# Attention scores as one float32 product each, from undivided queries and keys, in a kernel of attention, an MLP and a mixture of experts

## The chip, the cores and the metric

The kernel runs on one core of one Trainium2 chip. The metric is the device time of one execution in microseconds (us), the median of several runs. The engines are called as the profile calls them: PE (TensorE; PEld are its weight loads), DVE (VectorE), ACT (ScalarE), POOL (GpSimd) and SP (SyncE, which issues the DMAs).

## The reference

```python
# attention: q, k, v of (4, 8, 576, 64): batch, heads, positions, head width
scores = q @ k.transpose(0, 1, 3, 2) / np.sqrt(64)
scores = np.where(block_i >= block_j, scores, -1e9)      # blocks of 64 positions
attn = np.exp(scores - scores.max(-1, keepdims=True))
attn = attn / (attn.sum(-1, keepdims=True) + 1e-9)
x = (attn @ v).transpose(0, 2, 1, 3).reshape(2304, 512)
# MLP
h = x @ w_in                                             # 512 -> 2048
x = np.maximum(0.01 * h, h) @ w_out                      # 2048 -> 512
# mixture of 8 experts, every token through every expert
P = sinkhorn(np.exp(x @ w_gate - max))                   # 8 rounds, (2304, 8)
out = sum(P[:, e:e+1] * (np.maximum(x @ w1[e], 0) @ w2[e]) for e in range(8))
```

## The kernel before

Three stages follow one another on PE: attention, the MLP (`hidden`, `second`), and the experts (`product`, `combine`). Almost all products are made of float32r parts: an operand is divided into a high part (a rounded copy) and a low part (the rest), and a product is three matmuls: high with high, high with low, low with high. Only the transposes and the weighted sums of attention (`weigh`) and the small gate products multiply plain float32 tiles.

Attention goes through 16 pairs of heads. For each pair the queries and keys (`qraw`, `kraw`) come by DMA, and PE turns them (`turn_q`, `turn_k`, `turn_tail`: tiles `qm`, `km`, `qk_tail` in PSUM, all from one pool of three banks that the transposes `tr` of the weights share). ACT writes the high part and then DVE the low part of the turned operand: `spread` for the queries, scaled and laid out so that the two heads of a pair stand in a block diagonal (`qbdh`, `qbdl`), `split_k` for the keys (`kTh`, `kTl`). `score(p, i)` makes the scores of query block i, of both heads at once, against the first 64(i+1) keys: three matmuls into a PSUM tile `sc` (three banks), DVE takes the row maximum (`nmax`), ACT the exponentials (`ex`) with their sums. The last block, of 576 keys, is cut into two halves of 288. `normalise` scales the weights, `turn_attn` turns them (PE, then a copy `at` by ACT or DVE), and `weigh` multiplies them with the values into `av`.

The table `turns` puts beside each score of pair p+1 other work of pairs p-1 to p+3, and a scheduler that goes by a timeline model then sets the order of each engine's instructions. Between them stand the steps of `bits_steps`, which prepare the MLP's first weights on DVE, ACT and POOL (`wa`, `wb`, `wraw`).

Of the kernel before, what the change touches and what calls it, by code (L numbers as in the profile page):

```python
# [8 lines left out]
F32 = mybir.dt.float32  # L9
F32R = mybir.dt.float32r  # L10
U32 = mybir.dt.uint32
AF = mybir.ActivationFunctionType
ALU = mybir.AluOpType
AX = mybir.AxisListType

P = 128
BLK = 64
# [10 lines left out]
def f32(ap):  # L28
    return ap.bitcast(F32)
# [7 lines left out]
def block_attention_mlp_moe(  # L37
# [15 lines left out]
    nc = tc.nc  # L53
    B, H, S, D = q.shape
# [3 lines left out]
    NQ = S // BLK  # L58
# [7 lines left out]
    TAIL = S - NFULL * P  # L66
# [151 lines left out]
    def attention(att, ps_sc, ps_tr, ps_av):  # L218
# [1 line left out]
        kraw = att.tile([P, NKC, P], F32, name="kraw")  # L220

        vraw = [att.tile([P, NKC, P], F32, name=f"vraw{i}") for i in range(2)]
        qbd = [[att.tile([P, NQ, P], F32R, name=f"qbd{n}{i}") for n in "hl"] for i in range(2)]
        kT = [[att.tile([P, S], F32R, name=f"kT{n}{i}") for n in "hl"] for i in range(2)]
        nch = [(i + 2) // 2 for i in range(NQ)]
        off = [P * sum(nch[:i]) for i in range(NQ)]
        ew = P * sum(nch)
# [36 lines left out]
        W = NFULL * P  # L264

        def spread(p, src, lo, n):
            qh, ql = qbd[p % 2]
            scale = 1.0 / float(D) ** 0.5
            for h in range(2):
                r = slice(h * D, (h + 1) * D)  # L270
                to = (r, slice(lo, lo + n), slice(h * BLK, (h + 1) * BLK))
                x = src[r, 0:n * BLK].rearrange("p (n c) -> p n c", c=BLK)
                nc.scalar.activation(out=qh[to], in_=x, func=AF.Copy, scale=scale)  # L273
                nc.vector.scalar_tensor_tensor(
                    out=ql[to], in0=x, scalar=scale, in1=f32(qh[to]), op0=ALU.mult, op1=ALU.subtract
                )

        def split_k(p, src, lo, hi):
            kh, kl = kT[p % 2]
            nc.scalar.copy(out=kh[:, lo:hi], in_=src)  # L280
            nc.vector.tensor_tensor(out=kl[:, lo:hi], in0=src, in1=f32(kh[:, lo:hi]), op=ALU.subtract)

        def turn_q(p):
            qm = ps_tr.tile([P, 512], F32, name="qm", tag="tr")
            for t in range(NFULL):
                nc.tensor.transpose(qm[:, t * P:(t + 1) * P], qraw[:, t, :], ident)  # L286
            spread(p, qm, 0, W // BLK)

        def turn_k(p):
            km = ps_tr.tile([P, 512], F32, name="km", tag="tr")  # L290
            for t in range(NFULL):
                nc.tensor.transpose(km[:, t * P:(t + 1) * P], kraw[:, t, :], ident)
            split_k(p, km[:, 0:W], 0, W)

        def turn_tail(p):
            tail = ps_tr.tile([P, 512], F32, name="qk_tail", tag="tr")
            for s, raw in enumerate((qraw, kraw)):
                nc.tensor.transpose(
                    tail[:, s * TAIL:(s + 1) * TAIL], raw[:TAIL, NFULL, :], ident[:TAIL, :TAIL]
                )  # L300
            spread(p, tail, W // BLK, TAIL // BLK)
            split_k(p, tail[:, TAIL:2 * TAIL], W, S)

# [4 lines left out]

        def score(p, i):
            n = BLK * (i + 1)
            qh, ql = (t[:, i, :] for t in qbd[p % 2])
            kh, kl = kT[p % 2]
            cuts = [(0, n)] if n <= 512 else [(0, n // 2), (n // 2, n)]
            part = []
            nm, sm = nmax[p % 2], ssum[p % 2]
            x = col[i]
            for s, (lo, hi) in enumerate(cuts):
                sc = ps_sc.tile([P, 512], F32, name="sc", tag="sc")[:, 0:hi - lo]  # L320
                for m, (a, b) in enumerate(((qh, kh), (qh, kl), (ql, kh))):
                    nc.tensor.matmul(sc, a, b[:, lo:hi], start=m == 0, stop=m == 2)  # L322
                latest[0] = nc.vector.tensor_reduce(out=nm[:, x - s:x - s + 1], in_=sc, axis=AX.X, op=ALU.max, negate=True)  # L323
                part.append(sc)
            if len(cuts) > 1:
                nc.vector.tensor_tensor(out=nm[:, x:x + 1], in0=nm[:, x:x + 1], in1=nm[:, x - 1:x], op=ALU.min)
            for s, (lo, hi) in enumerate(cuts):
                nc.scalar.activation(  # L328
                    out=ex[p % 2][:, off[i] + lo:off[i] + hi], in_=part[s], func=AF.Exp,
                    bias=nm[:, x:x + 1], scale=1.0, accum_out=sm[:, x - s:x - s + 1],  # L330
                )
            if len(cuts) > 1:
                nc.gpsimd.tensor_tensor(out=sm[:, x:x + 1], in0=sm[:, x:x + 1], in1=sm[:, x - 1:x], op=ALU.add)
# [49 lines left out]
        def split_x(p):  # L383
# [4 lines left out]
            for u0, u1 in zip(cuts, cuts[1:]):  # L388
# [13 lines left out]
            [("cur", turn_attn, 2), ("nxt", load_v)],  # L402
            [("cur", turn_attn, 3), ("cur", weigh, 0, 0, 0), ("cur", weigh, 0, 1, 0),
             ("nxt", normalise, 0, 3), ("fol", turn_k), ("fol", turn_tail)],
            [("cur", weigh, 0, 0, 1), ("cur", weigh, 0, 1, 1)],
            [("cur", turn_attn, 4), ("cur", turn_attn, 5)],
# [4 lines left out]

        load_qk(0)
        nc.scalar.activation(out=ssum[0], in_=ident[:, 0:NQ + 1], func=AF.Exp)
        for t in qbd[0] + qbd[1]:
            nc.gpsimd.memset(f32(t), 0.0)
        for t in vraw:
            nc.gpsimd.memset(t[:, NFULL, :], 0.0)
        for t in ex:
            for i in range(0, NQ, 2):
                nc.gpsimd.memset(t[:, off[i] + BLK * (i + 1):off[i] + P * nch[i]], 0.0)  # L420
        turn_q(0)
        turn_k(0)
        turn_tail(0)
        load_qk(1)
        units = [(1, f) for f in range(FC)] + [(2, f) for f in range(2)]
        steps = []
        starts = [int(n * 1.4) for n in range(len(units))]
        for p in range(-1, NP + 1):
            who = {"prv": p - 1, "cur": p, "nxt": p + 1, "fol": p + 2}
            if p in starts:  # L430
                bits_load(*units[starts.index(p)])
            if p - 1 in starts:
                steps += bits_steps(*units[starts.index(p - 1)])
            if 0 <= p < NP:
                normalise(p, 6, 9)
            for i, beside in zip(turn_order, turns):
                if p + 1 < NP:
                    score(p + 1, i)
                for w, f, *a in beside:
                    if 0 <= who[w] < NP:  # L440
                        f(who[w], *a)
                if steps and p + 1 < NP:
                    with tc.issue_after(latest[0].ins if hasattr(latest[0], "ins") else latest[0]):
                        steps.pop(0)()
                elif steps:
                    steps.pop(0)()
            if p + 3 < NP:
                load_qk(p + 3)
# [7 lines left out]
    n = 1  # L456
# [4 lines left out]
    for g in range(0, P, 32):  # L461
        r = slice(g, g + 32)
        nc.vector.tensor_tensor(out=ident[r, r], in0=ramp[r, :], in1=turned[r, :], op=ALU.is_equal)
    w2a = ctx.enter_context(tc.tile_pool(name="w2a", bufs=1))
    with (
        tc.tile_pool(name="att", bufs=1) as att,
        tc.tile_pool(name="ps_sc", bufs=3, space=bass.MemoryType.PSUM) as ps_sc,
        tc.tile_pool(name="ps_tr", bufs=3, space=bass.MemoryType.PSUM) as ps_tr,
        tc.tile_pool(name="ps_av", bufs=1, space=bass.MemoryType.PSUM) as ps_av,
    ):  # L470
        wpools[2] = [w2a]
        attention(att, ps_sc, ps_tr, ps_av)
# [456 lines left out]
    for n in range(0, NGR, 2):  # L929
        p, e, i = groups[n]  # L930
# [74 lines left out]
```

## Time and profile before

| what | value |
|---|---|
| median of 3 runs | 2155.08 us (2152.91 to 2155.52) |
| span of the profiled execution | 2155.8 us; no other time of this execution is listed |
| mean granted clock of TensorE | 0.997 |
| busy over the span | PE 98%, PEld 87%, DVE 68%, ACT 43%, POOL 23% |
| attention ends, the MLP's first product | at 255.0 us |

The span runs from the first to the last instruction of one execution. Busy times of matmuls contain the time in which the array still fills and empties behind the next one, so 98% is no measure of how full the array is. Durations in the rows further down are from this one execution.

### The profile page before, as it was taken

Reading aid. Unit: us, or ns where it says so; the run is one execution under the profiler, and the core shown is the slowest. Engines: PE = TensorE matmul, PEld = TensorE weight load, DVE = VectorE, ACT = ScalarE, POOL = GpSimd, SP = SyncE. Lnnn points to the kernel's source line nnn. Section 1 sums busy time; section 2 is a strip of 40 time slices with the busy share of each in tenths; the row PEclk is TensorE's granted clock in tenths of the full one; section 3 lists DMA queues with packets and bytes.
Section 4 is the critical chain, followed back from the end, with each engine's and each line's share of the span. In section 5 each row is a group of like instructions: output and inputs, shape, how many; then the busy total and the mean of one; then the engine's idle time right before and its main releaser. Section 6 shows DMA issues by size and latency. Waiting matters only on the chain.

```text
span 2155.8 us, 29413 instructions
## 1 busy us (share of the span) xinstructions
PE 2119.0 (98%) x10932; PEld 1865.1 (87%) x10932; DVE 1458.1 (68%) x2411; ACT 926.7 (43%) x1932; POOL 503.7 (23%) x589
## 2 busy tenths in 40 slices
PE   7989899999999999999999999999999999999999
PEld 5666688988899899899989988998899899989998
DVE  7888675653456866766678667666768676667665
ACT  6777522232334433443345344434444444344432
POOL 3344321110022212221222122212222221222120
PEclk9999999999999999999999999999999999999999
DMA  4333123230012122212222222122213221222120
GB/s 102 85 88 91 38 69 94 71 118 1 1 30 69 47 72 78 79 51 67 79 79 77 70 79 79 42 77 78 76 43 108 79 70 48 79 79 66 52 78 30
DMA packets 157248, 146.63 MB, mean 68 GB/s; under 512 B 62640, under 2 KB 126128, under 8 KB 157104
## 3 DMA queue, kind: packets, MB, share of 16 engines
q1 hardware_dynamic: 157104, 144.75, 22.7%
q8 instruction: 86, 1.41, 0.3%
q14 instruction: 58, 0.48, 0.1%
HBM read 135.81 MB, written 8.91 MB: 67 GB/s over the span
## 4 chain that ended last, share of the span: by engine, by line
PE 93%; DVE 5%; ACT 1%; issue 0%; DMA 0%; POOL 0%; SPq 0%; ACTq 0%; DVEq 0%
PE o L798 36%; PE h_ps L744 32%; PE h_ps L519 9%; PE o L548 9%; PE sc L322 2%; PE av L378 2%; PE tr L353 2%; DVE nmax L323 1%; DVE ex L346 1%; PE qm L286 0%; DVE w1l L702 0%; ACT at L360 0%; DVE wb L184 0%; ACT ex L328 0%; ACT qbdh L273 0%
## 5 line engine op out<-in xcount | busy, mean ns | idle before, releaser
L798 PE MATMUL o<-w2h,xhlate 128*128 128x512 f32 x1152 | 402.6, 390 | 0.0
L798 PE MATMUL o<-w2h,xllate 128*128 128x512 f32 x1152 | 401.6, 389 | 0.0
L685 POOL TENSOR_TENSOR wa<-wraw 128x256 f32<-128x256 f32 x96 | 89.0, 927 | 1251.3 <-DVE w1l L702 1200.5
L752 ACT COPY s<-h_ps 128x384 f32<-128x384 f32 x288 | 138.5, 481 | 540.1 <-PE h_ps L744 540.0
L761 DVE TENSOR_TENSOR c<-h_ps,s 128x384 f32<-128x384 f32 x288 | 155.6, 554 | 312.9 <-PE h_ps L744 302.6
L744 PE MATMUL h_ps<-xhS,w1h 128*128 128x384 f32 x768 | 257.1, 335 | 0.0
L744 PE MATMUL h_ps<-xlS,w1h 128*128 128x384 f32 x768 | 256.5, 334 | 0.0
L744 PE MATMUL h_ps<-xhS,w1l 128*128 128x384 f32 x768 | 256.5, 334 | 0.0
L798 PEld LDWEIGHTS o<-w2h,xllate 128*128 128x128 f32 x1152 | 216.2, 188 | 45.4
L798 PEld LDWEIGHTS o<-w2h,xhlate 128*128 128x128 f32 x1152 | 216.2, 188 | 43.4
L798 PE MATMUL o<-w2l,xhlate 128*128 128x512 f32 x576 | 224.7, 390 | 0.0
L798 PE MATMUL o<-w2l,xllate 128*128 128x512 f32 x576 | 224.4, 390 | 0.0
L811 DVE SCALAR_TENSOR_TENSOR xa<-o,pr,xa 128x512 f32<-128x512 f32 x264 | 189.1, 740 | 50.9 <-PE o L798 50.9
L744 PE MATMUL h_ps<-xhA,w1l 128*128 128x384 f32 x576 | 193.0, 335 | 0.0
L744 PE MATMUL h_ps<-xhA,w1h 128*128 128x384 f32 x576 | 193.0, 335 | 0.0
L744 PE MATMUL h_ps<-xlA,w1h 128*128 128x384 f32 x576 | 192.8, 335 | 0.0
L702 DVE TENSOR_TENSOR w1l<-wraw,w1h 128x512 fp32r<-128x512 f32 x192 | 172.9, 938 | 0.1
L702 DVE TENSOR_TENSOR w1l<-wa,w1h 128x512 fp32r<-128x512 f32 x192 | 160.8, 840 | 0.0
L767 ACT ACTIVATE xllate<-c 128x384 fp32r<-128x384 f32 x144 | 75.7, 526 | 183.7 <-DVE c L761 183.7
L132 DVE TENSOR_TENSOR w2l<-wraw,w2h 128x1024 fp32r<-128x1024 f32 x100 | 145.7, 1457 | 7.8 <-ACT w2h L131 7.8
L744 PEld LDWEIGHTS h_ps<-xlS,w1h 128*128 128x128 f32 x768 | 144.2, 188 | 0.0
L744 PEld LDWEIGHTS h_ps<-xhS,w1h 128*128 128x128 f32 x768 | 144.2, 188 | 0.0
(167 smaller groups left out, 4227.0 us busy)
## 6 DMA issues: line engine op xcount, KB each, us to landing
wraw<-in_moe_w_dram SPq DMA_DIRECT2D x192, 512.0 KB, 4.3
wraw<-in_moe_w_in_dram SPq DMA_DIRECT2D x16, 512.0 KB, 3.8
wraw<-in_moe_w_out_dram SPq DMA_DIRECT2D x16, 512.0 KB, 3.7
out_dram<-xa SPq DMA_DIRECT2D x18, 256.0 KB, 2.0
qraw<-in_q_dram SPq DMA_DIRECT2D x32, 128.0 KB, 2.5
kraw<-in_k_dram SPq DMA_DIRECT2D x32, 128.0 KB, 2.6
vraw<-in_v_dram SPq DMA_DIRECT2D x32, 128.0 KB, 2.8
s_in<-wa SPq DMA_DIRECT2D x8, 256.0 KB, 2.4
```

Of the source, the lines that this page charges most:

```text
L132: nc.vector.tensor_tensor(out=lo, in0=raw, in1=f32(hi), op=ALU.subtract)
L322: nc.tensor.matmul(sc, a, b[:, lo:hi], start=m == 0, stop=m == 2)
L519: nc.tensor.matmul(ps[:, 0:n], w[:, c, cols], x, start=c == 0 and s == 0, stop=c == KC - 1 and s == 2,)
L548: nc.tensor.matmul(o_ps[s][:, 0:n], w[:, cut], h[:, 0:n], start=f == 0 and m == 0, stop=f == FC - 1 and m == 2)
L685: nc.gpsimd.tensor_tensor(out=one[:, 0], in0=a21, in1=a22, op=ALU.add)
L702: nc.vector.tensor_tensor(out=lo, in0=x, in1=f32(hi), op=ALU.subtract)
L744: mm = nc.tensor.matmul(ps, w[:, c], x[:, c], start=first and c == 0 and s == 0, stop=c == 1 and s == 2, skip_group_check=True,)
L752: nc.scalar.copy(out=t, in_=bank[n, name][:, 0:HT])
L761: nc.vector.tensor_tensor(out=c, in0=x, in1=part[n, add], op=ALU.add)
L767: nc.scalar.activation(out=hi, in_=x, func=AF.Relu),
L798: mm = nc.tensor.matmul(o, h, w, start=m == 0, stop=m == 11)
L811: nc.vector.scalar_tensor_tensor(out=a, in0=o, scalar=pr[:, tt, e:e + 1], in1=a, op0=ALU.mult, op1=ALU.add)
```

## The change

The queries and keys are no longer divided. `qbd` and `kT` are one float32 tile each, twice, where there were a high and a low one. ACT copies the turned queries with their scale into `qbd`, DVE copies the turned keys into `kT` (`place_k`, in the place of `split_k`), and a score is one matmul of two float32 tiles.

```diff
--- before.py
+++ after.py
@@ -220,8 +220,8 @@
         kraw = att.tile([P, NKC, P], F32, name="kraw")
 
         vraw = [att.tile([P, NKC, P], F32, name=f"vraw{i}") for i in range(2)]
-        qbd = [[att.tile([P, NQ, P], F32R, name=f"qbd{n}{i}") for n in "hl"] for i in range(2)]
-        kT = [[att.tile([P, S], F32R, name=f"kT{n}{i}") for n in "hl"] for i in range(2)]
+        qbd = [att.tile([P, NQ, P], F32, name=f"qbd{i}") for i in range(2)]
+        kT = [att.tile([P, S], F32, name=f"kT{i}") for i in range(2)]
         nch = [(i + 2) // 2 for i in range(NQ)]
         off = [P * sum(nch[:i]) for i in range(NQ)]
         ew = P * sum(nch)
@@ -264,21 +264,15 @@
         W = NFULL * P
 
         def spread(p, src, lo, n):
-            qh, ql = qbd[p % 2]
             scale = 1.0 / float(D) ** 0.5
             for h in range(2):
                 r = slice(h * D, (h + 1) * D)
-                to = (r, slice(lo, lo + n), slice(h * BLK, (h + 1) * BLK))
+                to = qbd[p % 2][r, lo:lo + n, h * BLK:(h + 1) * BLK]
                 x = src[r, 0:n * BLK].rearrange("p (n c) -> p n c", c=BLK)
-                nc.scalar.activation(out=qh[to], in_=x, func=AF.Copy, scale=scale)
-                nc.vector.scalar_tensor_tensor(
-                    out=ql[to], in0=x, scalar=scale, in1=f32(qh[to]), op0=ALU.mult, op1=ALU.subtract
-                )
-
-        def split_k(p, src, lo, hi):
-            kh, kl = kT[p % 2]
-            nc.scalar.copy(out=kh[:, lo:hi], in_=src)
-            nc.vector.tensor_tensor(out=kl[:, lo:hi], in0=src, in1=f32(kh[:, lo:hi]), op=ALU.subtract)
+                nc.scalar.activation(out=to, in_=x, func=AF.Copy, scale=scale)
+
+        def place_k(p, src, lo, hi):
+            nc.vector.tensor_copy(out=kT[p % 2][:, lo:hi], in_=src)
 
         def turn_q(p):
             qm = ps_tr.tile([P, 512], F32, name="qm", tag="tr")
@@ -290,7 +284,7 @@
             km = ps_tr.tile([P, 512], F32, name="km", tag="tr")
             for t in range(NFULL):
                 nc.tensor.transpose(km[:, t * P:(t + 1) * P], kraw[:, t, :], ident)
-            split_k(p, km[:, 0:W], 0, W)
+            place_k(p, km[:, 0:W], 0, W)
 
         def turn_tail(p):
             tail = ps_tr.tile([P, 512], F32, name="qk_tail", tag="tr")
@@ -299,7 +293,7 @@
                     tail[:, s * TAIL:(s + 1) * TAIL], raw[:TAIL, NFULL, :], ident[:TAIL, :TAIL]
                 )
             spread(p, tail, W // BLK, TAIL // BLK)
-            split_k(p, tail[:, TAIL:2 * TAIL], W, S)
+            place_k(p, tail[:, TAIL:2 * TAIL], W, S)
 
 
 
@@ -310,16 +304,13 @@
 
         def score(p, i):
             n = BLK * (i + 1)
-            qh, ql = (t[:, i, :] for t in qbd[p % 2])
-            kh, kl = kT[p % 2]
             cuts = [(0, n)] if n <= 512 else [(0, n // 2), (n // 2, n)]
             part = []
             nm, sm = nmax[p % 2], ssum[p % 2]
             x = col[i]
             for s, (lo, hi) in enumerate(cuts):
                 sc = ps_sc.tile([P, 512], F32, name="sc", tag="sc")[:, 0:hi - lo]
-                for m, (a, b) in enumerate(((qh, kh), (qh, kl), (ql, kh))):
-                    nc.tensor.matmul(sc, a, b[:, lo:hi], start=m == 0, stop=m == 2)
+                nc.tensor.matmul(sc, qbd[p % 2][:, i, :], kT[p % 2][:, lo:hi], start=True, stop=True)
                 latest[0] = nc.vector.tensor_reduce(out=nm[:, x - s:x - s + 1], in_=sc, axis=AX.X, op=ALU.max, negate=True)
                 part.append(sc)
             if len(cuts) > 1:
@@ -411,8 +402,8 @@
 
         load_qk(0)
         nc.scalar.activation(out=ssum[0], in_=ident[:, 0:NQ + 1], func=AF.Exp)
-        for t in qbd[0] + qbd[1]:
-            nc.gpsimd.memset(f32(t), 0.0)
+        for t in qbd:
+            nc.gpsimd.memset(t, 0.0)
         for t in vraw:
             nc.gpsimd.memset(t[:, NFULL, :], 0.0)
         for t in ex:
```

Behind attention the instructions stand in the same order as before on all five queues. In attention the scheduler has placed them anew. On PE, the queue in the eighth pair whose tails are turned: before, with the high parts `kTh`, `qbdh` and the low parts `kTl`, `qbdl`:

```order
L322 MATMUL sc<-kTh_121,qbdh_117 128x256
L322 MATMUL sc<-kTl_122,qbdh_117 128x256
L322 MATMUL sc<-kTh_121,qbdl_118 128x256
L353 MATMUL tr<-ident,ex_126 128x128
L322 MATMUL sc<-kTh_121,qbdh_117 128x320
L322 MATMUL sc<-kTl_122,qbdh_117 128x320
L322 MATMUL sc<-kTh_121,qbdl_118 128x320
L378 MATMUL av<-at,vraw_116 64x320 x2
L378 MATMUL av<-at,vraw_116 64x192 x2
```

The same place of the changed kernel, where L313 is the score, L344 the transpose of the weights, L280 that of the queries and L369 the weighted sum:

```order
L313 MATMUL sc<-kT_119,qbd_117 128x256
L344 MATMUL tr<-ident,ex_122 128x128 x5
L280 MATMUL qm<-ident,qraw 128x128 x4
L313 MATMUL sc<-kT_119,qbd_117 128x320
L313 MATMUL sc<-kT_120,qbd_118 128x288 x2
L369 MATMUL av<-at,vraw_116 64x320 x2
L369 MATMUL av<-at,vraw_116 64x192 x2
```

Three rows have become one, and the next pair's first scores and the queries' transposes now stand ahead of the weighted sums of 320 and 192 columns. On DVE, between the scaling of the weights `ex` of one pair and the maxima of the next, before:

```order
L346 TENSOR_SCALAR ex_125<-ex_125,rsum_131 128x576
L346 TENSOR_SCALAR ex_125<-ex_125,rsum_131 128x512
L323 TENSOR_REDUCE nmax_127<-sc 128x1 x2
L281 TENSOR_TENSOR kTl_124<-km,kTh_123 128x512
L274 SCALAR_TENSOR_TENSOR qbdl_120<-qk_tail,qbdh_119 64x64
L339 RECIPROCAL rsum_131<-rsum_131 128x3
L346 TENSOR_SCALAR ex_125<-ex_125,rsum_131 128x448
L274 SCALAR_TENSOR_TENSOR qbdl_120<-qk_tail,qbdh_119 64x64
L323 TENSOR_REDUCE nmax_127<-sc 128x1 x2
L281 TENSOR_TENSOR kTl_124<-qk_tail,kTh_123 128x64
```

And in the changed kernel, where L275 is the copy of the keys, L314 the maximum, L330 the reciprocal and L337 the scaling:

```order
L337 TENSOR_SCALAR ex_121<-ex_121,rsum_127 128x576
L337 TENSOR_SCALAR ex_121<-ex_121,rsum_127 128x512
L314 TENSOR_REDUCE nmax_123<-sc 128x1
L275 COPY kT_120<-km 128x512
L314 TENSOR_REDUCE nmax_123<-sc 128x1
L330 RECIPROCAL rsum_127<-rsum_127 128x3
L275 COPY kT_120<-qk_tail 128x64
L337 TENSOR_SCALAR ex_121<-ex_121,rsum_127 128x448
L314 TENSOR_REDUCE nmax_123<-sc 128x1
```

The subtractions for `qbdl` are gone, and the copies of the keys stand where their subtractions stood.

## Rows read from the trace of the kernel before

**Rows 1.** Page, part 1: busy us, share of the span, instructions.

```profile
PE 2119.0 (98%) x10932; PEld 1865.1 (87%) x10932; DVE 1458.1 (68%) x2411; ACT 926.7 (43%) x1932; POOL 503.7 (23%) x589
```

**Rows 2.** Windows: stretch, its length, busy us (and instructions) by engine, clock.

```profile
24.20:230.00 205.80, 186.45 (x1223) 129.65 (x1222) 176.49 (x441) 158.21 (x473) 88.12 (x132) 0.98 0.33 81
122.00:136.00 14.00, 11.88 (x76) 9.47 (x76) 10.84 (x27) 9.62 (x30) 7.37 (x11) 0.88 0.30 79
...
136.00:150.00 14.00, 13.71 (x97) 9.87 (x96) 11.99 (x33) 11.38 (x35) 4.40 (x9) 1.00 0.28 64
...
262.00:300.00 38.00, 38.00 (x170) 31.45 (x169) 26.98 (x42) 12.34 (x21) 14.09 (x10) 1.00 0.24 70
```

**Rows 3.** Chain that ended last, 24.2 to 230 us, share by line.

```profile
by line: PE sc L322 18.0%; PE av L378 13.9%; PE tr L353 12.6%; DVE nmax L323 9.3%; DVE ex L346 5.6%; DVE wb L184 3.4%; ACT at L360 3.2%; DVE qbdl L274 3.0%; DVE at L362 2.9%; ACT qbdh L273 2.8%; PE qm L286 2.7%; ACT ex L328 2.5%; PE km L292
```

**Rows 4.** Waits, 24.2 to 230 us: total us, times, longest.

```profile
DVE nmax L323 <- PE sc L322: 21.1, 34, 1.7
...
PEld sc L322 <- ACT at L360: 9.3, 14, 0.7
...
ACT qbdh L273 <- DVE qbdl L274: 7.0, 8, 1.8
...
PEld av L378 <- DVE at L362: 5.9, 10, 1.1
```

**Rows 5.** Timeline of PE, 135.7 to 147.2 us: start, length, what.

```profile
137.05 0.97 PE L378 MATMUL av<-at,vraw 128*64 128x448 f32 x4
137.96 0.66 PE L353 MATMUL tr<-ident,ex 128*128 128x128 f32 x4
...
139.67 0.28 PE L322 MATMUL sc<-kTl,qbdh 128*128 128x256 f32 x1
139.79 0.27 PE L322 MATMUL sc<-kTh,qbdl 128*128 128x256 f32 x1
...
142.21 0.28 PE L322 MATMUL sc<-kTl,qbdh 128*128 128x64 f32 x1
142.32 0.28 PE L322 MATMUL sc<-kTh,qbdl 128*128 128x64 f32 x1
...
144.02 0.34 PE L378 MATMUL av<-at,vraw 128*64 128x64 f32 x4
144.28 0.33 PE L353 MATMUL tr<-ident,ex 128*128 128x128 f32 x1
...
144.68 0.40 PE L322 MATMUL sc<-kTl,qbdh 128*128 128x512 f32 x1
144.92 0.39 PE L322 MATMUL sc<-kTh,qbdl 128*128 128x512 f32 x1
```

**Rows 6.** Groups of PE up to 255 us: busy us, mean ns, idle before.

```profile
L378 PE MATMUL av<-at,vraw 128*64 128x448 f32 x128 | 31.1, 564 | 0.0
```

**Rows 7.** Groups of DVE, 24.2 to 230 us.

```profile
L274 DVE SCALAR_TENSOR_TENSOR qbdl<-qm,qbdh 64x512 fp32r<-64x512 f32 x27 | 18.5, 685 | 0.8
...
L281 DVE TENSOR_TENSOR kTl<-km,kTh 128x512 fp32r<-128x512 f32 x14 | 9.5, 677 | 0.7 <-ACT kTh L280 0.7
L362 DVE COPY at<-tr 128x512 f32<-128x512 f32 x13 | 8.9, 685 | 0.2
...
L274 DVE SCALAR_TENSOR_TENSOR qbdl<-qk_tail,qbdh 64x64 fp32r<-64x64 f32 x28 | 6.0, 214 | 1.4 <-ACT qbdh L273 0.9
```

**Rows 8.** Groups of ACT, 24.2 to 230 us.

```profile
L280 ACT CAST kTh<-km 128x512 fp32r<-128x512 f32 x14 | 8.6, 616 | 0.2 <-PE km L292 0.2
...
L280 ACT CAST kTh<-qk_tail 128x64 fp32r<-128x64 f32 x13 | 2.7, 209 | 3.2 <-DVE qbdl L274 3.1
```

**Rows 9.** Start: the memsets of line L415, and PE's first work.

```profile
L415 POOL MEMSET qbdl<- x2: 1079/1080/1082, 1.9 to 3.9; 128x1152 f32 x2
...
6.26 1.09 PE L286 MATMUL qm<-ident,qraw 128*128 128x128 f32 x4 [6.26 <-DVE ident L463]
```

**Rows 10.** The chain in order of time, 254 to 300 us.

```profile
254.98 9.52 PE h_ps L519 x41
```

## The prediction

> **What bounds the kernel now.** I began with the totals: TensorE (PE) is busy for 98% of the span, VectorE (DVE) for 68%, ScalarE (ACT) for 43% [rows 1]. That average hides two stages, so I read the windows next. From 262 us on PE is busy 38.00 of 38.00 us, DVE 26.98 and ACT 12.34; there only PE work counts, and the change touches none of it. In the attention stage, in the stretch from 24.2 to 230 us, PE is busy 186.45 of 205.8 us, DVE 176.49 and ACT 158.21 [rows 2]. No engine is at its limit there, and three are near it. So what the change is worth is decided between 0 and 255 us, and whatever time is won or lost there reaches the end unchanged, since the instructions behind attention stand in the same order on all five queues as before.
>
> Then the chain of waits in that stretch. It is shared: the score products of L322 hold 18.0% of it, the weighted sums 13.9%, the transposes 12.6%; DVE's five lines hold 9.3 + 5.6 + 3.4 + 3.0 + 2.9 = 24.2%, and ACT's three 3.2 + 2.8 + 2.5 = 8.5% [rows 3]. Of 205.8 us that is 37.0 us of scores, 49.8 us of DVE and 17.5 us of ACT. The list of waits says why DVE is in it: PE's score loads and weighted sums wait 9.3 and 5.9 us for copies by ACT and DVE, and ACT itself waits 7.0 us before the queries' high part [rows 4] and 3.1 us before that of the keys' tail [rows 8] for the low part of the queries, which DVE writes from the same PSUM tile that ACT reads. The stretch holds 14 of 16 head pairs (the 14 key tiles of 512 columns), 14.7 us each.
>
> **The change part by part.** *Score products on PE.* Before, a product is three float32r matmuls. In the stretch from 136 to 150 us, at the full clock (1.00 granted [rows 2], the 2.4 GHz level), they start 0.11 us apart at 64 columns, 0.12 at 256 and 0.24 at 512 [rows 5]: 0.47 ns a column, but never under 0.11 us. A head pair scores widths 64, 128, 192, 256, 288 (twice), 320, 384, 448 and 512. By that rule one pass over them is 0.11 + 0.11 + 0.11 + 0.12 + 0.135 + 0.135 + 0.15 + 0.18 + 0.21 + 0.24 = 1.50 us, three are 4.50 us.
>
> The trace has no native float32 product on the full array. The nearest row is the weighted sum of L378, which multiplies plain float32 tiles, 64 output rows a head. Each call is two records: 128 records of 448 columns [rows 6] for 2 calls times 2 heads times 16 pairs = 64. Four records of 564 ns lie in a piece of 0.97 us, so the two heads overlap; the group lasts from 137.05 to 137.96 us at 448 columns and from 144.02 to 144.28 us at 64 [rows 5]: 0.91 us against 0.26, so (0.91 - 0.26)/384 = 1.69 ns a column for one head's two records, and a fixed part that I take for the change of the tiling and leave out. If the heads run side by side, a full-array product costs these 1.69 ns a column; if they take turns on the array, half of it. I take 1.69, since the records overlap in pairs; the half is kept as the lower end. Two weight loads at 0.11 us set a floor of 0.22 us. The sum is 0.22 + 0.22 + 0.32 + 0.43 + 0.49 + 0.49 + 0.54 + 0.65 + 0.76 + 0.87 = 4.99 us: **+0.49 us a pair, +7.8 us over 16.** The narrow ones get cheaper (0.33 to 0.22 us), the wide ones dearer (0.72 to 0.87 us). At half the column price the four narrowest stand at the floor, the rest at 0.24 to 0.43 us; the sum would be 2.8 us, and the change would save 1.7 us a pair.
>
> The Trainium skill (FP8 and Floating Point Precision, section TensorE Precision Notes) counts four passes through the array for a true float32 product, which speaks against the change: one pass more than three. By columns alone that pass would cost 16 pairs x 2,880 columns x 0.47 ns = 21.7 us. The rows agree with four passes at wide products if the heads run side by side, and not with a price by columns alone at narrow ones, where a start every 0.11 us is the floor.
>
> How much of the 7.8 us lies on the path? L322 is 37.0 us of the chain where its products take 14 x 4.50 = 63 us, so 0.59 of them: **+4.6 us**, from nothing to 7.8 at the ends.
>
> *DVE.* The subtractions for the low part of the queries go: 27 of 685 ns and 28 of 214 ns, 24.5 us in the stretch [rows 7]. The key's subtraction (677 ns) becomes a copy of the same shape out of PSUM; the nearest row is the copy of L362 at 685 ns, so it costs nothing either way. DVE falls by 24.5 of 176.5, 13.9%. The part of it in the chain, 3.0% of 205.8 = 6.2 us, goes whole. The other 43.6 us of DVE in the chain are partly work and partly a queue that gets shorter; I take half of 13.9%, 3.0 us. **-9.2 us**, with ends 0 (all taken up by PE's longer products) and -14.
>
> *ACT.* The key's high part goes, 14 of 616 and 13 of 209 ns, 11.3 of 158.2 us or 7.1% [rows 8]. Of ACT's 17.5 us in the chain that is **-1.2 us**. Its waits for DVE's low part (10.1 us in two lines) go too; where they mattered they are in DVE's 6.2 us already. The key tile in PSUM is now released by one copy of 0.68 us where it was held for 0.62 + 0.68 us, which I count at nothing, as PE had other transposes' banks to use; if not, it adds to the gain.
>
> *Start.* Two memsets on GpSimd (1.08 us each) go, but the first transposes wait for the identity that DVE completes at 6.26 us [rows 9]: nothing. Without that cover it would be 2.2 us at most.
>
> **The sum.** In the stretch 4.6 - 9.2 - 1.2 = -5.8 us for 14 pairs, -6.6 us for 16. The profiled execution's span is 2155.8 us and the median of the runs 2155.1, so the two agree to 0.7 us, and I subtract from the median: **2148.5 us**, 0.3% less. A measurement of this kernel tells about 0.2%, 4.3 us, from no change.
>
> **Rivals.**
> (a) *PE takes it all (slower).* If PE is what holds the stage, DVE's relief makes idle time and the longer products come in full: +7.8 us, 2163 us, and more if the clock falls oftener: it stood at 0.88 in one window of 14 us [rows 2], which is 1.7 us lost. It decides if PE's 19.4 us of waiting in the stretch do not fall by at least the 7 us that its work grows. For it: PE has the largest share of the chain. Against: a quarter of the chain is DVE.
> (b) *They cancel.* The relief on the path is only the 6.2 us of the subtraction, PE's part is 4.6 us or more: within 0.2% of 2155.1.
> (c) *DVE was the bound.* PE's waits vanish: 186.45/14 + 0.49 = 13.8 us a pair against 14.7, 0.9 us times 16 = 14 us, 2141 us. For it: DVE is busy 12.6 us of a pair and ACT waits for it. Against: the order still has PE wait for maxima and exponentials, 21.1 us of DVE waiting for scores [rows 4] among them, which do not go, and longer products make that wait longer.
> (d) *The heads take turns in the old row.* Then the scores save 1.7 us a pair, 27 us over 16, of which DVE and ACT, next in line, let through perhaps the most: 2130 us. Against: the records overlap in pairs.
>
> **How the numbers follow.** Forecast (2143 to 2150.8) 0.38; (a) 0.22, all beyond 2159.4; (b) 0.25; (c) 0.12; (d) 0.03. Faster is the forecast with (c) and (d), 0.53; same 0.25; slower 0.22. The range reaches over (b) into (c) and (a): 2138 to 2163, leaving out some 0.08 below and 0.1 above. The forecast's own range is 2143 to 2150.8.
>
> **What would show it.** Each score product as two records, 0.87 us together at 512 columns and 0.22 at 64; no low part on DVE, whose busy time up to the end of attention falls by some 29 us, ACT's by 13; the first product of the next stage (L519 before) starting at about 248 us where it started at 254.98 [rows 10]; from there to the end the same duration within 1 us. Wrong: the products' records at another price; PE's waits that do not shrink, so that attention ends at 260 us; or a copy of the keys on which scores wait for longer than they did for the split. A new stretch at half clock in attention would add the 1.7 us of such a window.

## The result, and the profile after

The changed kernel takes 2136.06 us (median of 4 runs, 2135.2 to 2137.32), the kernel before 2154.07 us (4 runs, 2152.91 to 2155.52) on the same chip: ratio 0.9913 [0.9899, 0.9927], 0.9% faster. I had forecast 2148.5 us; the range's lower end was 2138. The profiled execution took 2137.32 us at a span of 2135.5 us. Every run listed with both has a time 1.8 us above its span, so the profiled execution of the kernel before (span 2155.8 us) took about 2157.6 us, 2.5 to 3.5 us above the medians of that kernel (2155.08 and 2154.07 us): the two profiles lie some 2 us further apart than the two medians, which differ by 18.0 us.

Totals, the line that answers to [rows 1]:

```profile
PE 2114.1 (99%) x10772; PEld 1842.6 (86%) x10772; DVE 1434.7 (67%) x2347; ACT 915.0 (43%) x1900; POOL 500.9 (23%) x587
```

They hardly move. The windows do: the first row holds the same 14 pairs as the 205.8 us of [rows 2], the second is the stretch from 122 to 136 us, in which the clock stood at 0.88 before, the third a piece of the stage behind attention.

```profile
24.20:210.00 185.80, 180.63 (x1069) 111.87 (x1067) 151.60 (x377) 144.93 (x435) 85.45 (x129) 0.99 0.37 90
122.00:136.00 14.00, 14.00 (x86) 8.89 (x85) 11.42 (x28) 10.25 (x31) 4.21 (x7) 1.00 0.30 67
...
242.00:280.00 38.00, 38.00 (x169) 31.45 (x169) 25.46 (x38) 11.53 (x19) 13.36 (x10) 1.00 0.23 70
```

A pair takes 185.8/14 = 13.3 us where it took 14.7. PE is idle for 5.2 us of the stretch where it was for 19.4. Behind attention PE is full as before, and the next stage starts at 234.28 us (chain of the changed kernel) where it started at 254.98 [rows 10]: the whole gain of this pair of executions, 20.7 us (20.3 in their spans), lies in attention.

```profile
234.28 9.52 PE h_ps L510 x41
```

The chain of the stretch by line, against [rows 3]:

```profile
by line: PE sc L313 31.3%; PE av L369 18.4%; PE tr L344 18.3%; DVE ex L337 4.9%; DVE nmax L314 3.4%; PE km L286 3.2%; DMA wraw<-in_moe_w_out_dram 2.7%; PE av L366 2.6%; PE qm L280 2.6%; ACT ex L319 1.4%; PE qk_tail L292 1.4%; issue 1.3%; PO
```

PE's three large lines hold 68.0% of it, where they held 44.5%; DVE's maxima fell from 9.3% to 3.4%, and its copies of the turned weights and its split of the next stage's weights (2.9% and 3.4% before) are not among the lines that the row still shows. The waits of the stretch (24.2 to 210 us, against [rows 4]; the last row is one of before that [rows 4] does not have):

```profile
DVE nmax L314 <- PE sc L313: 19.2, 32, 1.9
...
PEld sc L313 <- ACT ex L319: 11.6, 20, 2.2
...
PEld sc L313 <- ACT at L351: 7.0, 10, 0.7
...
PEld av L369 <- DVE at L353: 0.8, 2, 0.4
```

```profile
PEld sc L322 <- ACT ex L328: 5.5, 13, 1.6
```

DVE waits for scores about as long as before, 19.2 us where it was 21.1. The weight loads of the weighted sums wait 0.8 us for DVE's copies where they waited 5.9; those of the scores now wait longest for ACT's exponentials, 11.6 us where it was 5.5. A weight load that waits need not make PE idle: PE itself is idle for 5.2 us of this stretch.

The products' price, on PE's timeline from 140.0 to 141.5 us:

```profile
140.00 0.33 PE L313 MATMUL sc<-kT,qbd 128*128 128x64 f32 x2
140.17 0.28 PE L344 MATMUL tr<-ident,ex 128*128 128x128 f32 x1
140.29 1.02 PE L313 MATMUL sc<-kT,qbd 128*128 128x512 f32 x2
141.15 0.60 PE L344 MATMUL tr<-ident,ex 128*128 128x128 f32 x4
```

A product is two records (`x2`). The one of 512 columns holds the array from 140.29 to 141.15, 0.86 us; the summed price was 0.87. The one of 64 columns takes 0.17 us here (140.00 to 140.17), where 0.22 was summed. The Trainium skill (FP8 and Floating Point Precision, section TensorE Precision Notes) counts four passes for it; four passes at the 0.24 us between float32r records of 512 columns [rows 5] would be 0.96, so the row agrees nearly, at this width.

On DVE (groups of 24.2 to 210 us, against [rows 7]) the subtractions of the queries are gone, and the copy of the keys costs what the subtraction cost:

```profile
L275 DVE COPY kT<-km 128x512 f32<-128x512 f32 x14 | 9.5, 680 | 1.6 <-PE km L286 1.6
```

At the start PE's first work comes 0.9 us earlier than in [rows 9], which I had said it would not. DVE completes the identity earlier: from 3.00 us on, two of its small operations take 1.11 us (second row) where they took 2.01 us (third row, the kernel before). Before, GpSimd's four memsets of 128x1152 ran until 4.98 us, beside both operations; now there are two and they end at 2.94 us.

```profile
5.35 1.09 PE L280 MATMUL qm<-ident,qraw 128*128 128x128 f32 x4 [5.35 <-DVE ident L454]
```

```profile
3.00 1.11 DVE L449 TENSOR_SCALAR ramp<-ramp 128x8 f32<-128x8 f32 x2
```

```profile
3.00 2.01 DVE L458 TENSOR_SCALAR ramp<-ramp 128x8 f32<-128x8 f32 x2
```

The **budget** of attention is read from two windows, from 0 to the start of the next stage, before and after (the second ends at that stage's first record, 0.07 us ahead of its start in the chain):

```profile
0.00:254.98 254.98, 223.30 (x1425) 156.75 (x1425) 205.79 (x514) 183.43 (x543) 102.39 (x169) 0.97 0.34 83
```

```profile
0.00:234.21 234.21, 217.79 (x1265) 134.28 (x1265) 180.24 (x450) 172.19 (x511) 100.69 (x167) 0.99 0.37 91
```

PE's idle time falls from 31.7 to 16.4 us, and its busy time by 5.5 us although its products cost 7.8 us more by the summed price. A part of that is the clock. Before, it stood at 0.50 of its granted rate (the 1.2 GHz level) in four pieces of 3.4 us; after, in one. In a stretch of the same length ahead of each, PE had been idle for a good part (1.3 to 2.0 us before, 2.5 us after); here are one of before and the one of after, each with that stretch ahead of it:

```profile
127.80:131.20 3.40, 2.09 (x12) 1.41 (x11) 3.06 (x9) 3.12 (x10) 1.66 (x3) 1.00 0.66 150
...
131.20:134.60 3.40, 3.40 (x17) 3.16 (x15) 1.08 (x3) 2.58 (x7) 0.42 (x2) 0.50 0.02 5
```

```profile
195.60:199.00 3.40, 0.92 (x3) 0.59 (x4) 2.63 (x9) 1.53 (x6) 1.20 (x2) 1.00 0.19 44
...
199.00:202.40 3.40, 3.40 (x14) 2.72 (x13) 1.28 (x3) 1.65 (x6) 0.23 (x2) 0.50 0.00 0
```

At the other three places of before PE was busy for 1.66, 2.00 and 1.42 of the 3.4 us ahead. The trace's record of the clock begins at 18.6 us before and at 11.3 us after; until then four transposes take 1.05 to 1.09 us, where later ones take 0.60 to 0.66, so I count that time to the lower level too (the windows print 1.00 where there is no record). PE is busy 10.4 + 4 x 3.4 = 24.0 us at the lower level before and 5.3 + 3.4 = 8.7 us after; half of the difference, 7.6 us, is an estimate of the time given back, if the same work takes half as long at the full clock. So -20.8 = -15.3 of idle time + 7.8 of products - 7.6 of clock - 5.7 that I can't itemise. This is the budget of one pair of executions: the mean clock of the kernel before goes from 0.996 to 0.999 from one execution to another, so the pieces at the lower level are not the same in each.

### The profile page after: what moved, and what is told of

Read it like the earlier page. It is cut to its first block, busy times and chain, and to the rows that moved or that the text cites. A ratio compares the mean times of both kernels' runs of the same rounds, so it can differ in the third digit from the quotient of the medians.

```text
span 2135.5 us, 29009 instructions
## 1 busy us (share of the span) xinstructions
PE 2114.1 (99%) x10772; PEld 1842.6 (86%) x10772; DVE 1434.7 (67%) x2347; ACT 915.0 (43%) x1900; POOL 500.9 (23%) x587
## 4 chain that ended last, share of the span: by engine, by line
PE 95%; DVE 3%; ACT 1%; issue 0%; DMA 0%; POOL 0%; SPq 0%; ACTq 0%; POOLq 0%; DVEq 0%
PE o L789 36%; PE h_ps L735 33%; PE o L539 9%; PE h_ps L510 9%; PE sc L313 3%; PE av L369 2%; PE tr L344 2%; DVE ex L337 0%; DVE w1l L693 0%; DVE nmax L314 0%; PE km L286 0%; ACT ex L319 0%; PE qm L280 0%; PE av L366 0%; DMA wraw<-in_moe_w_out_dram 0%
```

## The experiments

Three theories stood at the start. The first: **DVE's load** is what counts, its 25 us fewer make nearly the whole gain, and the products cost something. The second: **the product itself** gains, since a score waits for one copy of queries and keys and not for a low part behind it. The third: **the clock**, which falls less often if PE idles less or has more to do. Where an expectation uses letters, R and R1 are the first, W is the second, C the third, and P takes the second and third together; R2 is a variant of the first, in which not DVE's load counts but its place between two of ACT's steps on one PSUM tile. Each ratio is against the kernel before on the same chip.

| kernel | us | ratio [95%] |
|---|---|---|
| e1, products alone | 2151.84 | 0.9980 [0.9971, 0.9989] |
| e2, relief alone | 2140.10 | 0.9923 [0.9908, 0.9938] |
| e3, one float32r pass | 2118.1 | 0.9823 [0.9808, 0.9838] |
| e4, keys copied by ACT | 2134.15 | 0.9898 [0.9881, 0.9914] |
| e5, before, PE busy at the start | 2155.0 | 0.9992 [0.9983, 1.0001] |
| e6, e4 and PE busy at the start | 2134.33 | 0.9892 [0.9876, 0.9909] |
| e7, DVE's load back | 2158.29 | 1.0009 [0.9999, 1.0018] |
| e8, the changed kernel again | 2135.41 | 0.9903 [0.9889, 0.9918] |
| e9, half of e7's load | 2148.74 | 0.9976 [0.9966, 0.9985] |
| e10, before, no subtraction of keys | 2147.13 | 0.9961 [0.9946, 0.9976] |
| e11, after, more PE work | 2152.41 | 0.9987 [0.9977, 0.9997] |
| e12, e4 again | 2134.38 | 0.9904 [0.9890, 0.9919] |
| e13, before, more PE work | 2160.64 | 1.0026 [1.0016, 1.0035] |
| e14, e2, more PE work | 2135.88 | 0.9909 [0.9894, 0.9924] |

### The two halves: e1, e2, and e3

e1 takes the native product and keeps DVE's and ACT's work as it was; the low parts go to tiles that nobody reads.

```diff
+                low = qlow[p % 2][r, lo:lo + n, h * BLK:(h + 1) * BLK]
+                nc.vector.scalar_tensor_tensor(out=low, in0=x, scalar=scale, in1=to, op0=ALU.mult, op1=ALU.subtract)
...
-            nc.vector.tensor_copy(out=kT[p % 2][:, lo:hi], in_=src)
+            full = kT[p % 2][:, lo:hi]
+            nc.scalar.copy(out=full, in_=src)
+            nc.vector.tensor_tensor(out=klow[p % 2][:, lo:hi], in0=src, in1=full, op=ALU.subtract)
```

> Scores as one native float32 product each, but DVE and ACT keep all the divided work: ACT copies queries and keys, DVE subtracts, and the low parts that result are read by nobody. Theory R (the 20 us come from the work that DVE and ACT lost): PE's longer products come without the relief, 2152 to 2162 us, at or above the kernel before. Theory P (one float32 product in the place of three keeps PE denser, its clock up, and frees it from waiting for the low parts): most of the gain stays, 2136 to 2142 us.

e2 drops the low parts and keeps three float32r passes, here three times the same product with a third of the scale; it leaves out what the low parts add to the scores. e3 is e2 with one pass and the whole scale.

```diff
+                for m in range(3):
+                    nc.tensor.matmul(sc, qbd[p % 2][:, i, :], kT[p % 2][:, lo:hi], start=m == 0, stop=m == 2)
```

> The relief alone: queries and keys are copied once, by ACT and DVE as in the changed kernel, and a score is three float32r matmuls of the same two tiles with a third of the scale, so PE's work is that of the kernel before and the low parts' share of the scores is left out. Theory R: below the changed kernel by about PE's price of the native products, 0.49 us times 16 pairs = 7.8 us, so 2126 to 2131 us. Theory P: back to about the kernel before less the small relief on the path, 2146 to 2155 us.

> The changed kernel with one float32r matmul for a score instead of one float32 product (the low parts' share of the scores is left out): PE has 4.99 - 1.50 = 3.49 us less a pair. If PE alone now holds attention, 16 times that, 56 us, goes: 2080 us. If DVE and ACT are close behind, as R says with DVE busy 180 of 235 us and ACT 173, a good part of it does not come: 2100 to 2122 us.

Their windows from 0 to the end of attention, e1, e2, e3:

```profile
0.00:249.56 249.56, 225.28 (x1265) 134.46 (x1265) 203.40 (x514) 183.09 (x543) 106.00 (x167) 1.00 0.35 85
```

```profile
0.00:237.60 237.60, 217.49 (x1425) 157.51 (x1425) 176.14 (x450) 173.06 (x511) 101.88 (x167) 0.96 0.37 90
```

```profile
0.00:217.03 217.03, 186.26 (x1105) 118.26 (x1105) 173.31 (x450) 169.45 (x511) 103.72 (x167) 0.94 0.40 98
```

The parts add up: 0.9980 x 0.9923 = 0.9903, the ratio of e8. The relief alone is worth 0.77%, 16.6 us; that lies between what the two theories had said for e2. It came although the clock was no higher than before: 0.96 in the window, and a mean of 0.996 over e2's runs against 0.997. The products alone, with DVE's 203 us of load kept, do not cost time, they save 0.2% (4.3 us; interval 2.4 to 6.3), and 2151.84 us lies just below R's range. In e1 PE's idle time is 24.3 us against 31.7 before, and the window's clock is 1.00 where it was 0.97: 2 us more of busy time, not 7.8. The clock is up in all ten runs of e1, 0.999 to 1.000 against 0.996 to 0.998.

Where PE's idle time went shows in its groups up to the end of attention, all widths together: the transposes of the weights before and in e1, then the scores before (two of their three passes) and in e1.

```profile
L353 PE MATMUL tr<-ident,ex 128*128 128x128 f32 x400 | 72.0, 295 | 15.2 <-ACT ex L344 6.8 <-ACT at L360 4.7 <-POOL ex L346 1.4
```

```profile
L350 PE MATMUL tr<-ident,ex 128*128 128x128 f32 x400 | 63.4, 280 | 8.2 <-ACT ex L341 5.1 <-ACT at L357 2.2 <-DVE klow L281 0.4
```

```profile
L322 PE MATMUL sc<-kTh,qbdh 128*128 128x288 f32 (+8 forms) x160 | 60.3, 380 | 3.4 <-ACT ex L328 2.5 <-ACT qbdh L273 0.6
...
L322 PE MATMUL sc<-kTh,qbdl 128*128 128x288 f32 (+8 forms) x160 | 51.5, 322 | 1.2 <-DVE qbdl L274 1.2
```

```profile
L319 PE MATMUL sc<-kT,qbd 128*128 128x288 f32 (+8 forms) x320 | 106.4, 439 | 5.0 <-ACT ex L325 3.0 <-ACT qbd L274 0.9 <-ACT kT L280 0.5
```

Ahead of the scores PE is idle for 4.6 us before and 5.0 in e1, and only 1.2 of the 4.6 were a wait for a low part. Of the 7.4 us that e1 loses, 7.0 lie ahead of the transposes.

e3 shows how much PE held: 31 us of its busy time less than in e2 make 20.6 us of attention, with the clock down to 0.94.

### DVE's load: e7 (with e8 beside it) and e9

e7 is the changed kernel with the two subtractions of the queries put back as work alone: DVE reads the finished tile in SBUF and writes to one that nobody reads, so it holds no PSUM tile and no score needs it. e9 does so for one head of two (the second line under `if h == 0`).

```diff
+                low = busy[r, lo:lo + n, h * BLK:(h + 1) * BLK]
+                nc.vector.scalar_tensor_tensor(out=low, in0=to, scalar=scale, in1=to, op0=ALU.mult, op1=ALU.subtract)
```

> The changed kernel with DVE's load put back but not its place between ACT and PE: after each copy of the queries DVE subtracts within SBUF into a tile that nobody reads, so no PSUM tile is held by it and ACT does not wait for it. Theory R1 (DVE's hours count: 24.5 us in the stretch and 28 over attention): most of the relief goes, 2146 to 2152 us. Theory R2 (the chain ACT, DVE, ACT on one PSUM tile counts, not DVE's load): 2136 to 2140 us.

> The changed kernel itself, on the same chip as the variants: 2135 to 2137 us, so that a variant with the keys by ACT can be set against it.

> Half of the load that went back onto DVE in the variant with DVE kept busy: the subtraction within SBUF for one head of a pair, 0.686 + 0.294 us a pair, some 15 us over attention. If the stage's time goes with DVE's load all the way (theory R1), half of the 22 us: 2145 to 2149 us. If there is a point up to which DVE's load is hidden behind PE: 2136 to 2141 us.

DVE's groups that e7 adds, its chain by line from 24.2 to 230 us, and the windows of e7 and e9 up to the end of attention:

```profile
L275 DVE SCALAR_TENSOR_TENSOR busy<-qbd 64x512 fp32r<-64x512 f32 x32 | 21.9, 686 | 4.3 <-ACT qbd L273 3.8
...
L275 DVE SCALAR_TENSOR_TENSOR busy<-qbd 64x64 fp32r<-64x64 f32 x32 | 9.4, 294 | 0.4
```

```profile
by line: PE sc L316 15.0%; DVE ex L340 11.1%; DVE nmax L317 11.0%; PE tr L347 10.3%; DVE busy L275 8.3%; PE av L372 6.1%; ACT ex L322 4.8%; issue 4.4%; ACT ex L338 3.6%; DVE wb L184 3.0%; DVE at L356 2.6%; ACT at L354 2.5%; ACT qbd L273 2.4
```

```profile
0.00:254.30 254.30, 224.58 (x1265) 136.64 (x1265) 208.83 (x514) 172.89 (x511) 97.41 (x167) 0.98 0.34 84
```

```profile
0.00:248.91 248.91, 224.97 (x1265) 136.16 (x1265) 191.98 (x482) 172.78 (x511) 102.47 (x167) 0.99 0.35 85
```

31.3 us of DVE's time that nothing reads take the whole gain away: 2158.29 against 2135.41 us on that chip, 22.9 us, or 0.73 us for each of them. That is more than R1 had said (2146 to 2152 us), and R2 is refuted. Half of it (e9) takes 0.73% away, from 0.9903 to 0.9976, more than half of the 1.06%: for DVE's busy time in the windows, 15.7 us for the first 11.7 and 7 us for the next 16.8, so no single price holds along the way. This is load: these instructions hold no PSUM tile and no score needs their result, and they stand in the chain themselves with 8.3%, in front of what follows them in DVE's queue. PE's idle time is back at 29.7 us in e7, and the mean clock of its runs is 0.997 where e8's is 0.999, so a part of the 22.9 us may come by way of the clock.

### The same relief from before: e10

e10 is the kernel before without the subtraction for the keys' low part; that part is zero from the start and PE multiplies it still. It leaves out what that part adds to the scores.

```diff
-            nc.vector.tensor_tensor(out=kl[:, lo:hi], in0=src, in1=f32(kh[:, lo:hi]), op=ALU.subtract)
...
+        for t in kT:
+            nc.gpsimd.memset(f32(t[1]), 0.0)
```

> The kernel before without the subtraction that makes the keys' low part, 14.3 us of DVE; the low part is zero, so its share of the scores is left out, and PE still multiplies with it. Theory R1 by the price of the relief alone (16.6 us for 29.7 us less on DVE): 8 us less, 2147 to 2150 us where the kernel before has 2154 to 2157. My prediction's price (half of DVE's share): 3 to 4 us less.

```profile
0.00:245.31 245.31, 218.68 (x1425) 158.08 (x1425) 192.82 (x482) 181.81 (x543) 104.51 (x171) 0.97 0.35 87
```

13 us off DVE give 0.39%, 8.4 us, 0.65 us for each, from the other kernel; by the same windows e2's 16.6 us for 29.7 are 0.56 and e7's 22.9 for 28.6 are 0.80. PE executes what it did before, at the same clock of 0.97, and still its busy time is 4.6 us shorter (218.7 against 223.3). In e2, with as many matmuls and the clock at 0.96, it is 5.8 us shorter. So with less on DVE not only PE's idle time shrinks; these are amounts like the 5.7 us that the budget left over, and no row here shows why. e10 takes away a wait along with the load, since no score needs a subtraction of the keys any more and the turned keys' PSUM tile is free after ACT's copy; e7, which adds load alone, does not have this rival.

### Is PE the bound now? e11, e4 and e12

e11 adds a product with a zero tile behind each score of 512 columns, 16 x 0.87 us of PE's time. e4 and e12 (the same kernel) take the keys' copies off DVE and give them to ACT.

```diff
+                if wide:
+                    nc.tensor.matmul(sc, zero, kT[p % 2][:, lo:hi], start=False, stop=True)
```

```diff
-            nc.vector.tensor_copy(out=kT[p % 2][:, lo:hi], in_=src)
+            nc.scalar.copy(out=kT[p % 2][:, lo:hi], in_=src)
```

> The changed kernel with a second product of 512 columns behind the one of block 7, with zeros as its stationary tile, so that nothing else changes: 0.87 us more of PE a pair, 13.9 us over 16. If PE now holds attention (its part of the chain grew from 142 to 171 us): 2145 to 2150 us. If PE still has room (as the native products' 7.8 us seemed to cost nothing): 2136 to 2141 us.

> The changed kernel with ACT in the place of DVE copying the turned keys: 14.3 us move from DVE to ACT over attention. If DVE's load is what counts (theory R in its narrow form), faster by 1 to 5 us, 2131 to 2135. If ACT's queue counts as much, same or slower, 2136 to 2142 us. Theory P: no change, 2135 to 2137 us.

> The variant with the keys copied by ACT once more, against the changed kernel's 2135.4 and 2136.1 us: 2133 to 2135 us if its small lead is real, 2135 to 2137 if it was chance.

Windows up to the end of attention, e11 and e12:

```profile
0.00:247.03 247.03, 232.26 (x1297) 140.38 (x1297) 174.96 (x450) 173.63 (x511) 102.17 (x168) 0.99 0.35 86
```

```profile
0.00:230.30 230.30, 215.28 (x1264) 134.08 (x1264) 163.60 (x418) 181.25 (x543) 101.03 (x167) 1.00 0.38 92
```

13.9 us of PE's time cost 0.84% (0.9903 to 0.9987), 18 us: here a longer product comes in full and more. The score of 512 columns also ends 0.87 us later for DVE and ACT, so this is the price of PE's time and of that delay together. In e4 and e12 16.6 us go from DVE, but ACT gets 9.1 us more (172.2 to 181.3), so they do not price DVE's relief alone; together the two changes are worth little: 2134.2 and 2134.4 us against 2136.1 and 2135.4, a lead of 1 to 2 us that the intervals don't tell from nothing. Among the kernels with the native product and no added work on PE the end of attention goes with DVE's busy time: 163.6, 180.2, 192.0, 203.4 and 208.8 us on DVE (e12, after, e9, e1, e7) end at 230.3, 234.2, 248.9, 249.6 and 254.3 us. These are single executions, and the step from e9 to e1 shows how loose the relation is: 11.4 us of DVE for 0.7 us.

### The clock and the order: e5, e6, e13, e14

e5 gives the kernel before two float32 products of ones at the start, e6 gives them to e4. e13 adds, to the kernel before, a fourth float32r pass with a zero tile at 448 and 512 columns, 7.2 us in all; e14 adds the same to e2. e13 thus has about the changed kernel's work on PE and the old waits; neither filler changes a score.

```diff
+        warm = att.tile([P, 512], F32, name="warm")
+        nc.gpsimd.memset(warm, 1.0)
+        cold = ps_sc.tile([P, 512], F32, name="cold", tag="sc")
+        for m in range(2):
+            nc.tensor.matmul(cold, warm[:, 0:P], warm, start=True, stop=True)
```

```diff
+                if hi - lo >= 448:
+                    nc.tensor.matmul(sc, zero, kh[:, lo:hi], start=False, stop=True)
```

> The kernel before with two float32 products of 512 columns on a tile of ones at its start, while PE waits for the identity; nothing reads them. If the granted clock in attention costs what its rows say (PE is busy for 10.4 us at the lower level before 18.6 us), the clock rises earlier and up to 4 us go: 2150 to 2153 us where the kernel before has 2154 to 2157. If the clock does not matter there (the waits for DMA and for DVE set the start): no change.

> The changed kernel with the keys copied by ACT, and the same two products at the start. If the start's clock matters, 1 to 3 us below the variant with the keys by ACT (2134.2), where PE is busy for 7.4 us at the lower level: 2131 to 2133 us. If not, 2134 us.

> The kernel before with one more float32r pass, with zeros as its stationary tile, behind the three of widths 448 and 512: 0.21 + 0.24 us a pair, 7.2 us over 16, nearly what the native products add, and nothing else is changed. If a denser PE pays for itself through the clock (theory C), the mean clock rises from 0.997 to 0.999 or more and the time stays, 2152 to 2157 us. If what paid in the variant with PE's part alone was that no score waits for a low part any more (theory W), the clock stays and the time grows: 2158 to 2164 us.

> The relief alone with the same filler, 7.2 us of PE more than the relief alone had (2140.1 us at a clock of 0.996). Theory C: the clock rises and the time stays at 2136 to 2142 us, as it did in the changed kernel, whose native products add 7.8 us. Theory W: PE holds the stage there, nothing else changes, and the 7 us come: 2145 to 2149 us.

Windows up to the end of attention, e13 and e14:

```profile
0.00:256.75 256.75, 224.72 (x1457) 160.00 (x1457) 202.23 (x514) 184.39 (x543) 102.42 (x170) 0.99 0.34 83
```

```profile
0.00:230.56 230.56, 215.17 (x1457) 157.74 (x1457) 177.40 (x450) 172.03 (x511) 101.23 (x168) 1.00 0.37 92
```

e5 and e6 show no gain beyond the intervals. In e5 the clock rose at 7.6 us and was down again from 11.1 us, so what an earlier rise is worth stays open. In e13 the filler costs 0.26%, 5.6 us (interval 3.4 to 7.5), as W had said, and the mean clock of its ten runs, 0.9975, is hardly above the 0.9972 of the kernel before; the 0.99 of the window is that of one execution. So more work on PE alone did not raise the clock, and a longer score did cost time in the kernel with 31.7 us of idle time on PE. PE's idle time is 32.0 us in e13, as before, and 24.3 in e1.

e1's gain therefore needs more than a busier PE, and this is as far as the runs go. It comes with the higher clock, 0.0024 in the mean of the runs; by e8's runs (further down) a thousandth goes with 1.3 to 3.5 us, so the clock can be enough for all of the 4.3 us. The higher clock may follow from the shorter idle time, but why that is shorter ahead of the transposes is not shown: the scores' own wait for the low part itself was 1.2 us. The scheduler places attention anew for each kernel here, so an effect of some us may be one of order, and no run takes that apart. In e14 the same useless work did not slow e2 down (0.9923 to 0.9909, 3 us less, and the intervals overlap): W's 2145 to 2149 us did not come there. The mean clock of e14's runs is 0.998 where e2's was 0.996.

## Why the prediction was wrong

**Products' price: right at the wide end.** 0.86 us at 512 columns where 0.87 was summed, 0.17 at 64 where it was 0.22; the old row of the weighted sum was the right neighbour, heads side by side.

**"How much of the 7.8 us lies on the path?": the step that failed, wrong in sign.** It put +4.6 us for the products into the sum, +5.3 over 16 pairs; e1 measured -4.3 with DVE's load kept, so this term is off by 9.6 us. The share of the chain was not what was wrong: e13 prices a longer score alone at 5.6 us for 7.2, 0.78 for one (0.5 to 1.0 by its interval), where 0.59 was taken. What was wrong is that length was all that the term counted. That one product in the place of three would change PE's waits and clock was put at nothing on the gain's side; e1 shows 7.4 us less of idle time on PE, nearly all of it ahead of the transposes, and the clock at 0.9996 where the kernel before had 0.9972. Why these came stays open (order, or the earlier scores).

A slip in the sum goes beside it and changes little: the 4.6 us are 0.59 of the 7.8 us of all 16 pairs, but stand in a sum for 14 pairs that is then brought to 16. With 0.59 of 6.9 us the sum is -7.3 instead of -6.6 us.

**"I take half of 13.9%, 3.0 us. -9.2 us": mis-sized.** With ACT's 1.2 us this was 11.9 us over 16 pairs; e2 measured 16.6. A microsecond of DVE's time was worth 0.56 (e2), 0.65 (e10) and 0.73 to 0.80 (e7), where 9.2/24.5 = 0.38 was taken. The chain put DVE at 24%. That the instructions of PE and ACT in it had waited in turn for something behind DVE's queue is an explanation that no row here shows; to put DVE's load back is what told its worth.

**Rival (c), "DVE was the bound", came nearest**, with a chance of 0.12 and a price of 14 us, 2141 us. Its direction was right, its sum was luck in part: PE's waits did not vanish (19.4 us in the stretch fell to 5.2, 31.7 in attention to 16.4), and PE's busy time, which it let grow by the products, fell by 5.5 us. In the profiled pair the clock fell to its lower level once in place of four times and rose earlier at the start; the note that it might fall oftener named only the loss. Nor was DVE the bound alone: its time was worth less than one for one in e2, e10 and e7, and PE's cost 0.78 for one in e13. Rivals (a), (b) and (d) did not come: attention did not end later, the change is clear of noise, and the product's row is not half as dear.

**The signs.** DVE's busy time up to the end of attention fell by 25.6 us (29 were said), ACT's by 11.2 (13); the next stage starts at 234.28 us and not at 248; the stage behind attention took 1901 us in both, as predicted.

**Start: wrong by 0.9 us**, since DVE's identity itself came earlier. **The profile's 2155.8 us** is a span; with the 1.8 us between a span and its time it does not agree with the median to 0.7 us but lies 2.5 above it, which moves the forecast by nothing, since it was taken from the median.

What stays open: what makes the clock fall, beyond PE's idle time ahead of each piece; why PE idled less in e1; and how much of a few us is the order alone.

## What to carry to other kernels

In a stage where three engines are each busy for 77 to 91%, a share of the chain priced an engine's work too low: 0.38 for DVE where the runs gave 0.56 to 0.80. Put useless work of the suspected size on that engine (e7) and take the difference. Do it in the kernel before too, for the engine that gets more work: idle time on PE did not make a longer score free (e13, 5.6 us for 7.2). And price apart what a change does to the waits and what it does to the length: here the same products gave 4.3 us back (e1), and one sum over lengths could not have shown it. Look at the mean clock of all runs and not of the profiled one alone, since it can differ between variants by as much as the effect.

## What the runs showed of the hardware

More work on PE has no fixed price: 7.2 us of useless float32r passes cost 5.6 us in e13 and nothing in e14, and 13.9 us of useless products cost 18 us in e11. The profiled executions of e2 and e14 show the clock's side of it: attention ended at 237.6 us at a clock of 0.96 in the window and at 230.6 us at 1.00, with 7.2 us more work; but e14's was the fastest of four, and the ratios differ by less than their intervals, so that useless work shortens a kernel is not shown. Executions of one kernel go with the mean clock too: e8's four took 2139.6 us at a mean granted clock of 0.998, 2136.0 at 0.999, and 2134.6 and 2134.8 at 1.000, so 1.3 to 3.5 us go with a thousandth. And small operations of VectorE took longer while GpSimd's memsets of 128x1152 ran: two of them 2.01 us beside them and 1.11 us behind them.
